# ScalarE's share of a weight conversion, put behind the ScalarE work that stands ahead of it in the source

## The chip, the cores and the metric

One core of a Trainium2 chip runs the whole program. The metric is device time in microseconds (us), the median of several runs; a lower time is better. The core has five engines that work side by side, each through its own list of instructions in the order in which it was given: TensorE (PE in the profile; its weight loads are PEld), VectorE (DVE), ScalarE (ACT), GpSimd (POOL) and SyncE (SP), which here only issues DMA transfers.

## The reference, cut to what matters

Retention over 4 batches, 8 heads, 576 positions of 64 elements, then two feed-forward layers over 2304 tokens. The four weight matrices come as 64-bit floats and are converted on the chip; the other inputs are float32.

```python
scores = q @ k.T / sqrt(64)
x = (scores * (gamma ** (i - j) where i >= j else 0)) @ v   # 2304 x 512
h = x @ moe_w_in                                            # 512 -> 2048
g = where(h > 0, h, exp(min(h, 0)) - 1)
x = g @ moe_w_out                                           # 2048 -> 512
h = maximum(x @ moe2_w_in, 0)
out = (h * h) @ moe2_w_out
```

## The kernel before, in words

**Tokens and steps.** The 2304 tokens are five blocks of 512, 512, 256, 512 and 512. The 2048 hidden columns are 16 slices `f` of 128. A step (layer, block, f) is an `up` (12 matmuls, which make `h` for one slice) and, two steps later (`LAG`), a `down` (12 matmuls, which add that slice's part to four accumulators `acc`). Each product is three matmuls (lines 130 to 132), since every operand is split into a high and a low half: ScalarE's cast (line 126) makes the high half, VectorE's subtraction (line 127) the low one. In layer one, blocks 0 and 1 take turns in three groups of slices: block 0 with f = 0 to 5, block 1 with f = 0 to 5, block 0 with f = 6 to 10, and so on; these 32 steps use each weight slice twice. The third operation behind an `up` is ScalarE's Tanh (line 314); behind it VectorE makes `t` (lines 316, 317), and ScalarE and VectorE split it into `g`, which the `down` needs.

**Weights.** A unit is one slice of one of the two matrices of a layer, 32 units in layer one (list `w1`). `load_raw` brings it in, `to_f32` converts it with two ScalarE operations (lines 160, 161) and four VectorE ones (162, 163, 164, 167), and `split_w` splits it with one cast on ScalarE and one subtraction on VectorE. `w1_to(n)` carries this on until n units are split; the source calls it after each piece of the first block's attention (`EARLY`) and in `mid`, in the middle of each `up`, behind the Tanh, with n from `units1(i)`: 7 units, then 1.4 a step, then 0.85 a step.

**Attention.** A chunk of up to 128 positions goes through `transposes` (PE line 239, then ScalarE's copies, line 244), `scores` (PE 252, then VectorE's masking, 255) and `values` (PE 267 and 271, then `x` is split, lines 126 and 127; PE 281 and VectorE 287 or 289 carry the state `st` on). `scale_chunk` is VectorE's line 214. Block 1 has five chunks: one of 64 positions (done ahead of the steps or beside the first), three of 128, of which the first starts a batch, and one of 64. `SPREAD` places their pieces in the source in the first five steps. They share two PSUM buffers (`ps_a`) and one set of `qT`, `kT`, `P0`, `P1`, and each chunk needs the state of the one before, so they follow each other nearly in series. The first `up` of block 1 needs all five.

**What sets the order.** The source is in this order, but a scheduler lays the instructions of each engine out anew when the program is built, by its own estimate of when each could start. It keeps what data needs, and edges that the source adds: `tc.issue_after(ins)` puts ScalarE's instructions of its block behind `ins`, if that is one of ScalarE's, in ScalarE's list. The conversion of layer two's weights already stands in such a block (behind `mark[0]`, the last Tanh); that of layer one doesn't.

Of the kernel before, what the change touches and what calls it, by code (L numbers as in the profile page):

```python
# [98 lines left out]
def tile_kernel(ctx: ExitStack, tc, q, k, v, w_in1, w_out1, w_in2, w_out2, cst, out):  # L99
    nc = tc.nc  # L100
# [36 lines left out]
    def load_raw(layer, which, f):  # L137
        w = ((w_in1, w_out1), (w_in2, w_out2))[layer][which].bitcast(I32)
        if layer == 0:

            t = wp.tile([P, DM, 2], I32, tag=f"w{which}_{f}", name="raw")
        else:
            t = raw_p.tile([P, DM, 2], I32, tag="raw", name="raw")
        if which == 0:
            nc.sync.dma_start(
                out=t.rearrange("p (k f) t -> p k (f t)", k=KC),
                in_=w[:, 2 * f * P:2 * (f + 1) * P].rearrange("(k p) f -> p k f", p=P),
            )
        else:
            nc.sync.dma_start(out=t.rearrange("p c t -> p (c t)"), in_=w[f * P:(f + 1) * P, :])  # L150
        raws[layer, which, f] = t
# [229 lines left out]
    w1 = [(0, *u) for u in units]  # L381
# [8 lines left out]
    at = dict(load=0, scale=0, next=0, raw=0, f32=0, split=0, raw2=0, f322=0, park=0, fetch=0, split2=0)  # L390
# [26 lines left out]
    def step(name, limit, todo_, work):  # L417
        if at[name] < min(limit, len(todo_)):
            work(todo_[at[name]])
            at[name] += 1  # L420

    def w1_to(n):

        while at["split"] < min(int(n), len(w1)):
            while at["raw"] < min(at["f32"] + AHEAD, len(w1)):
                step("raw", 99, w1, lambda u: load_raw(*u))
            step("split", at["f32"], w1, split_w)
            step("f32", at["raw"], w1, to_f32)
# [14 lines left out]
    for (c, piece), n in zip(pieces, EARLY):  # L443
        first[c][piece]()
        w1_to(n)
        if piece == 0 and c < 2:
            scale_next()
        if (c, piece) in ((0, 2), (2, 2)):
            load_next()
# [5 lines left out]
    for i, (layer, blk, f) in enumerate(steps):  # L455
        def mid():
            for of, (lo, hi) in SPREAD.items():
                if lo <= i < hi:
                    need = 3 * len(blocks[of])
                    for _ in range((i - lo + 1) * need // (hi - lo) - (i - lo) * need // (hi - lo)):  # L460
                        attn_step()
            if at["split"] < len(w1):
                w1_to(units1(i))
            elif layer == 0 and i >= SHARED and at["f322"] < min(len(w2), units2(i)):

                step("park", at["f322"], w2, park_w)
                with tc.issue_after(mark[0]):
                    step("f322", at["raw2"], w2, to_f32)
                while at["raw2"] < min(len(w2), at["f322"] + 2):
                    step("raw2", 99, w2, lambda u: load_raw(*u))  # L470
# [19 lines left out]
        if (layer, f) == (0, 1) and blk == NB - 1 or (layer, f) == (1, LAG) and blk < NB - 1:  # L490
            n = blk + 1 if layer else 0
# [30 lines left out]
```

## Time and profile before

| | |
|---|---|
| median of 3 runs | 946.06 us (943.92 to 947.9) |
| profiled execution: its time, and its span from the first to the last instruction | 946.56 us, 944.8 us |
| mean granted clock of TensorE, as a share of 2.4 GHz | 0.977 |
| busy in the span: PE, PEld, DVE, ACT | 906.6, 753.2, 506.9, 423.3 us |
| DMA, over the span | 97.47 MB, mean 103 GB/s |

The profile gives one execution. Busy time is time within instructions; those of one engine can overlap a little, so that the time that an engine needs for one more instruction is read from start to start of instructions that follow each other without a gap. Matmul ends are modelled. A mean over the span hides stages with other limits, so the stretches are read one by one.

### The profile page before, as it was taken

What the parts mean: (1) busy time and instruction counts of PE and PEld (TensorE: products, weight loads), DVE (VectorE), ACT (ScalarE), POOL (GpSimd) and SP (SyncE); (2) the same over time, 40 slices, a digit from 0 to 9 for tenths busy, and PEclk for the clock granted to TensorE, in tenths of its full rate; (3) what the DMA queues carried; (4) which work ended last, traced back from release to release, by engine and by line L of the source; (5) the groups of instructions that cost most, each with busy time, mean ns of one, the idle gap of its engine ahead of it and who ended that gap; (6) DMA issues with size and microseconds to landing.
All of it is one profiled execution on the core that took longest, in us unless ns stands there. A gap on an engine that the chain in (4) does not pass through costs nothing.

```text
span 944.8 us, 12423 instructions
## 1 busy us (share of the span) xinstructions
PE 906.6 (96%) x4934; PEld 753.2 (80%) x4934; DVE 506.9 (54%) x890; ACT 423.3 (45%) x770; POOL 9.3 (1%) x12
## 2 busy tenths in 40 slices
PE   7798589999998999999999999999999999999997
PEld 5676577887788998888788888888888988888886
DVE  5899995354557878767787642223223332223222
ACT  4797464544555666565767632222222222223221
POOL 3000000000000000000000000000000000000000
PEclk9889599999998999999999999999999999999999
DMA  9995230222148567433854530011003020001001
GB/s 230 297 369 137 46 89 1 89 90 89 45 123 253 161 168 218 139 125 110 289 196 140 153 137 1 1 44 45 1 1 134 1 112 1 1 1 45 1 1 44
DMA packets 97081, 97.47 MB, mean 103 GB/s; under 512 B 59264, under 2 KB 77824, under 8 KB 96512
## 3 DMA queue, kind: packets, MB, share of 16 engines
q1 hardware_dynamic: 97024, 96.69, 33.6%
q8 instruction: 38, 0.62, 0.3%
q14 instruction: 19, 0.16, 0.1%
HBM read 69.94 MB, written 26.74 MB: 102 GB/s over the span
## 4 chain that ended last, share of the span: by engine, by line
PE 83%; DVE 12%; DMA 2%; issue 1%; ACT 0%; SPq 0%; POOL 0%; DVEq 0%
PE acc L130 13%; PE acc L131 13%; PE h L130 13%; PE acc L132 13%; PE h L132 13%; PE h L131 13%; DVE f L164 2%; DVE f L167 2%; DVE w L127 2%; PE ps_o L271 2%; PE ps_s L252 1%; DVE f L162 1%; PE ps_o L267 1%; DVE f L163 1%; PE ps_t L239 1%
## 5 line engine op out<-in xcount | busy, mean ns | idle before, releaser
L130 PE MATMUL h<-x,w 128*128 128x512 f32 (+1 forms) x640 | 239.4, 375 | 3.8 <-DVE t L317 3.8
L131 PE MATMUL h<-x,w 128*128 128x512 f32 (+1 forms) x640 | 237.3, 371 | 0.0
L132 PE MATMUL h<-x,w 128*128 128x512 f32 (+1 forms) x640 | 237.1, 370 | 0.0
L321 DVE SCALAR_TENSOR_TENSOR t<-h,t 128x512 f32<-128x512 f32 (+1 forms) x80 | 51.1, 639 | 230.0 <-ACT t L319 230.0
L319 ACT ACTIVATE t<-h 128x512 f32<-128x512 f32 (+1 forms) x80 | 44.4, 555 | 237.2 <-PE h L132 237.2
L130 PEld LDWEIGHTS h<-x,w 128*128 128x128 f32 x640 | 122.0, 191 | 27.0 <-DVE t L317 5.3
L126 ACT CAST g<-t 128x512 fp32r<-128x512 f32 (+1 forms) x160 | 92.4, 578 | 110.1 <-DVE t L321 52.1
L127 DVE TENSOR_TENSOR g<-t,g 128x512 fp32r<-128x512 f32 (+1 forms) x160 | 102.1, 638 | 70.9 <-ACT g L126 64.8
L131 PEld LDWEIGHTS h<-x,w 128*128 128x128 f32 x640 | 122.0, 191 | 21.2 <-DVE x L127 0.4
L132 PEld LDWEIGHTS h<-x,w 128*128 128x128 f32 x640 | 121.7, 190 | 20.3
L131 PE MATMUL acc<-g,w 128*128 128x512 f32 (+1 forms) x320 | 118.7, 372 | 1.2 <-DVE g L127 1.2
L132 PE MATMUL acc<-g,w 128*128 128x512 f32 (+1 forms) x320 | 118.0, 370 | 0.0
L130 PE MATMUL acc<-g,w 128*128 128x512 f32 (+1 forms) x320 | 113.5, 378 | 0.0
L130 PE MATMUL acc<-w,g 128*128 128x512 f32 x288 | 112.2, 390 | 0.0
L131 PE MATMUL acc<-w,g 128*128 128x512 f32 x288 | 112.2, 390 | 0.0
L132 PE MATMUL acc<-w,g 128*128 128x512 f32 x288 | 111.6, 389 | 0.0
L316 DVE SCALAR_TENSOR_TENSOR t<-e,t 128x512 f32<-128x512 f32 (+1 forms) x80 | 50.9, 636 | 74.5 <-ACT t L314 74.5
L312 ACT ACTIVATE t<-h 128x512 f32<-128x512 f32 (+1 forms) x80 | 44.2, 553 | 85.7 <-PE h L132 81.7
L131 PEld LDWEIGHTS acc<-g,w 128*128 128x128 f32 x320 | 60.2, 188 | 11.8 <-DVE g L127 1.9
L130 PEld LDWEIGHTS acc<-g,w 128*128 128x128 f32 x320 | 59.3, 188 | 11.6 <-issue 0.9
L132 PEld LDWEIGHTS acc<-g,w 128*128 128x128 f32 x320 | 60.3, 188 | 10.3
L132 PEld LDWEIGHTS acc<-w,g 128*128 128x128 f32 x288 | 54.1, 188 | 11.4
(65 smaller groups left out, 936.1 us busy)
## 6 DMA issues: line engine op xcount, KB each, us to landing
raw<-in_moe_w_in_dram SPq DMA_DIRECT2D x32, 512.0 KB, 5.7
raw<-in_moe_w_out_dram SPq DMA_DIRECT2D x32, 512.0 KB, 5.9
x2s<-x SPq DMA_DIRECT2D x16, 512.0 KB, 3.6
w2s<-f SPq DMA_DIRECT2D x32, 256.0 KB, 2.3
x<-x2s SPq DMA_DIRECT2D x4, 2048.0 KB, 8.4
f<-w2s SPq DMA_DIRECT2D x32, 256.0 KB, 2.7
out_dram<-o SPq DMA_DIRECT2D x18, 256.0 KB, 2.5
parts<-part SPq DMA_DIRECT2D x8, 512.0 KB, 2.8
```

The lines of the kernel that those rows point to most:

```text
L126: nc.scalar.copy(pair_hi, src)
L127: eng.tensor_tensor(out=pair_lo, in0=src, in1=pair_hi.bitcast(F32), op=ALU.subtract)
L130: nc.tensor.matmul(ps, l_hi, r_hi, start=first, stop=False)
L131: nc.tensor.matmul(ps, l_hi, r_lo, start=False, stop=False)
L132: nc.tensor.matmul(ps, l_lo, r_hi, start=False, stop=last)
L164: nc.vector.scalar_tensor_tensor(out=ai, in0=upper, scalar=-(1 << 31), in1=ai, op0=ALU.bitwise_and, op1=ALU.bitwise_or)
L167: nc.vector.tensor_tensor(out=ai, in0=ai, in1=lower, op=ALU.add)
L271: nc.tensor.matmul(ps[e * D:(e + 1) * D, p, :n], vn[:n, 2 * p + e, :], live[e][:n, p, :n], start=not s, stop=True, skip_group_check=True,)
L312: nc.scalar.activation(t, h, AF.Relu, scale=-1.0)
L316: nc.vector.scalar_tensor_tensor(out=t, in0=e, scalar=1.0, in1=t, op0=ALU.add, op1=ALU.mult)
L319: nc.scalar.activation(t, h, AF.Relu)
L321: nc.vector.scalar_tensor_tensor(out=t, in0=h, scalar=0.0, in1=t, op0=ALU.max, op1=ALU.mult)
```

## The change

Whenever a call of `w1_to` has something to do, all that it issues stands in an `issue_after` block behind the last ScalarE instruction that the source has issued by then. In `mid` that is the Tanh of this step's `up`, or, since the attention's pieces are issued ahead of it there, the last ScalarE operation of those. Nothing is added or taken away on any engine: each has as many instructions as before.

```diff
+    def last_act():
+        return next(i for i in reversed(nc.cur_bb.bb.instructions) if i.engine == mybir.EngineType.Activation)
+
     def w1_to(n):
 
+
+        if at["split"] < min(int(n), len(w1)):
+            with tc.issue_after(last_act()):
+                w1_run(n)
+
+    def w1_run(n):
         while at["split"] < min(int(n), len(w1)):
             while at["raw"] < min(at["f32"] + AHEAD, len(w1)):
                 step("raw", 99, w1, lambda u: load_raw(*u))
```

What the scheduler makes of it is seen in the engines' lists. Names are those of tiles; in `w_5_958` the 5 is the slice, and the last number counts tiles. ScalarE from the first split of an `x` of block 1's attention on, first as it was ahead of and around the split of `w_3_627` (slice 3 of the second matrix):

```order
L161 ACTIVATE f<-raw 128x512
L160 ACTIVATE raw<-raw 128x512
L126 CAST w_4_534<-f 128x512
L160 ACTIVATE raw<-raw 128x512
L126 CAST g<-t 128x512
L160 ACTIVATE raw<-raw 128x512
L161 ACTIVATE f<-raw 128x512
L312 ACTIVATE t<-h 128x512
L160 ACTIVATE raw<-raw 128x512
L313 ACTIVATE e<-t 128x512
L126 CAST w_3_627<-f 128x512
```

and the same place, up to the same split, now:

```order
L126 CAST g<-t 128x512
L314 ACTIVATE t<-t 128x512
L312 ACTIVATE t<-h 128x512
L126 CAST g<-t 128x512
L313 ACTIVATE e<-t 128x512
L314 ACTIVATE t<-t 128x512
L126 CAST g<-t 128x512
L312 ACTIVATE t<-h 128x512
L313 ACTIVATE e<-t 128x512
L126 CAST x<-ps_o 128x4x128
L126 CAST w_3_627<-f 128x512
```

Conversions (lines 160 and 161) of later slices stood between the steps' own operations; now three steps' own operations and a chunk's `x` come ahead of them. VectorE has no edge of its own, but its list follows. The end of block 1's attention there, up to the low half of its last `x`, before:

```order
L255 TENSOR_TENSOR P_918<-ps_s,cs 64x4x64
L255 TENSOR_TENSOR P_920<-ps_s,cs 64x4x64
L214 TENSOR_TENSOR q<-q,cs 128x512
L167 ISA f<-raw,f 128x1024
L162 TENSOR_SCALAR f<-f 128x512
L127 TENSOR_TENSOR w_10_1487<-f,w_10_1487 128x512
L163 TENSOR_SCALAR f<-f 128x512
L127 TENSOR_TENSOR w_12_1534<-f,w_12_1534 128x512
L164 SCALAR_TENSOR_TENSOR f<-raw,f 128x512
L162 TENSOR_SCALAR f<-f 128x512
L127 TENSOR_TENSOR x<-ps_o,x 128x4x64
```

and now:

```order
L127 TENSOR_TENSOR w_6_849<-f,w_6_849 128x512
L162 TENSOR_SCALAR f<-f 128x512
L127 TENSOR_TENSOR g<-t,g 128x512
L163 TENSOR_SCALAR f<-f 128x512
L214 TENSOR_TENSOR k<-k,cs 128x512
L164 SCALAR_TENSOR_TENSOR f<-raw,f 128x512
L255 TENSOR_TENSOR P_918<-ps_s,cs 64x4x64
L255 TENSOR_TENSOR P_920<-ps_s,cs 64x4x64
L167 ISA f<-raw,f 128x1024
L214 TENSOR_TENSOR q<-q,cs 128x512
L127 TENSOR_TENSOR x<-ps_o,x 128x4x64
```

The same `x` now comes when slice 6 is being split, where it came when slice 12 was. On TensorE, behind the first two `up` of block 1 (`w_0_217`, `w_1_269`) there now stands block 0's `down` of slice 5, which stood ahead of block 1's first `up` before:

```order
L132 MATMUL h<-x,w_1_269 128x512
L130 MATMUL h<-x,w_1_269 128x512
L131 MATMUL h<-x,w_1_269 128x512
L132 MATMUL h<-x,w_1_269 128x512
L130 MATMUL acc_750<-g,w_5_958 128x512
L131 MATMUL acc_750<-g,w_5_958 128x512
```

Its twelve matmuls moved past the two `up`. All lists are as before again from about the 32nd step on.

## Rows read from the trace of the kernel before

**Rows 1.** The page, busy us (share of the span) and instructions of three engines.
```profile
PE 906.6 (96%) x4934; PEld 753.2 (80%) x4934; DVE 506.9 (54%) x890; ACT 423.3 (45%) x770; POOL 9.3 (1%) x12
```

**Rows 2.** Windows: start:end, length, busy us (instructions) per engine, granted clock, DMA.
```profile
core 0: us, PE busy (x) PEld busy (x) DVE busy (x) ACT busy (x) POOL busy (x), PEclk, DMA share, GB/s
44.70:117.70 73.00, 56.24 (x392) 45.11 (x390) 72.77 (x142) 52.90 (x97) 0.00 (x0) 0.82 0.63 191
46.00:88.00 42.00, 37.16 (x198) 28.73 (x199) 41.92 (x81) 36.38 (x67) 0.00 (x0) 0.92 0.85 265
88.00:117.00 29.00, 17.20 (x173) 14.99 (x171) 28.85 (x58) 15.04 (x28) 0.00 (x0) 0.69 0.31 82
116.90:132.00 15.10, 12.54 (x65) 9.97 (x64) 14.99 (x31) 9.66 (x18) 0.00 (x0) 0.92 0.33 71
146.00:288.00 142.00, 142.00 (x710) 115.42 (x709) 70.53 (x113) 68.09 (x119) 0.00 (x0) 1.00 0.26 80
318.00:456.00 138.00, 138.00 (x935) 117.33 (x931) 103.22 (x198) 84.78 (x163) 0.00 (x0) 1.00 0.54 161
```

**Rows 3.** Timeline of VectorE: start us, us, engine, line, operation, tiles, form, count.
```profile
44.71 0.68 DVE L164 SCALAR_TENSOR_TENSOR f<-raw,f 128x512 int32<-128x512 int32 x1
...
113.92 0.68 DVE L167 CUSTOM_DVE_ANT_0 f<-raw,f 128x1024 uint16<-128x1024 uint16 x1
114.52 0.41 DVE L162 TENSOR_SCALAR f<-f 128x512 f32<-128x512 f32 x1
114.86 0.68 DVE L127 TENSOR_TENSOR w<-f,w 128x512 fp32r<-128x512 f32 x1
...
117.33 0.41 DVE L127 TENSOR_TENSOR x<-ps_o,x 128x256 fp32r<-128x256 f32 x1
```

**Rows 4.** Timeline of TensorE, 46 to 118 us; in brackets idle time before, and its releaser.
```profile
46.13 0.63 PE L239 MATMUL ps_t<-cs,q 128*128 128x128 f32 x4 [0.25 <-DVE q L214]
...
69.84 0.39 PE L131 MATMUL acc<-g,w 128*128 128x512 f32 x1
70.07 0.39 PE L132 MATMUL acc<-g,w 128*128 128x512 f32 x1
...
83.66 1.16 PE L252 MATMUL ps_s<-qT,kT 64*128 64x128 f32 x16
...
88.56 1.06 PE L267 MATMUL ps_o<-qT,st 128*128 128x128 f32 x8
...
90.47 0.64 PE L281 MATMUL ps_u<-v,k 128*64 128x64 f32 x16
92.92 0.66 PE L239 MATMUL ps_t<-cs,q 128*128 128x128 f32 x4 [1.82 <-DVE x L127]
...
95.92 2.08 PE L252 MATMUL ps_s<-qT,kT 64*128 64x128 f32 x16 [1.51 <-ACT kT L244]
100.75 2.08 PE L267 MATMUL ps_o<-qT,st 128*128 128x128 f32 x8 [2.75 <-DVE P L255]
...
104.53 1.07 PE L281 MATMUL ps_u<-v,k 128*64 128x64 f32 x16
107.17 0.46 PE L239 MATMUL ps_t<-cs,q 64*128 64x64 f32 x4 [1.58 <-DVE x L127]
...
116.93 1.22 PE L130 MATMUL h<-x,w 128*128 128x512 f32 x2
```

**Rows 5.** Timeline of ScalarE, two conversions and a cast in a stretch without gaps.
```profile
52.10 0.69 ACT L160 ACTIVATE raw<-raw 128x512 int32<-128x512 uint32 x1
52.67 0.62 ACT L126 CAST w<-f 128x512 fp32r<-128x512 f32 x1
53.17 0.73 ACT L160 ACTIVATE raw<-raw 128x512 int32<-128x512 uint32 x1
```

**Rows 6.** Waits, 46 to 146 us: waiter, releaser, us in total, times, longest.
```profile
ACT w L126 <- DVE f L167: 10.0, 7, 3.4
```

## The prediction, made before the changed kernel was run

> **What bounds the kernel now.** I read the page's busy shares first, then windows of successive stretches, then the timelines of the stretch that stands out. By the page TensorE is the bound: 906.6 of 944.8 us busy, VectorE half idle [rows 1]. The windows say when that holds: from 146 to 288 us and from 318 to 456 us TensorE is busy without a gap, at a granted clock of 1.00 [rows 2]. It doesn't hold early. From 88 to 117 us TensorE is busy 17.2 of 29 us, at a mean granted clock of 0.69, so partly at the lower of its two levels (1.2 instead of 2.4 GHz), and VectorE is busy 28.85 of 29; from 44.7 to 117.7 us VectorE is busy 72.77 of 73.0 us [rows 2]. There VectorE is the bound, and the reader should ask what it is busy with.
>
> The timeline of TensorE shows what is waited for. From 92.92 us on it does only block 1's attention, chunk after chunk, at 14.25 us each (92.92 to 107.17), and stands idle in front of the transposes for VectorE's `x`, and in front of `ps_o` for VectorE's `P` (2.75 us); only at 116.93 us does block 1's first `up` begin [rows 4]. It reads the last `x`, whose low half VectorE makes at 117.33 us [rows 3]. So all that VectorE does ahead of that `x` delays TensorE, and part of it needn't be there: the lists show conversions of slices 6 to 12, while block 1's first six steps use slices 0 to 5.
>
> **What the change moves.** No instruction is added or removed. The lists of before and after are the same on VectorE up to the operation that starts at 44.71 us [rows 3]. From that place up to the last `x` of block 1, VectorE has 140 instructions before and 80 after. All but the weight conversions agree: 11 scalings, 8 maskings, 6 of state, 5 `x` and 18 for `t` and `g` in both. The 60 that moved behind are 13 of line 162, 12 of 163, 12 of 164, 11 of 167 and 12 of line 127 on weights. From start to start a full-size operation takes 0.60 us (113.92 to 114.52) and a line 162 takes 0.34 (114.52 to 114.86) [rows 3]; line 163 is like 162. So 35 x 0.60 + 25 x 0.34 = 29.5 us of VectorE's work leave the stretch, and 73.0 - 29.5 = 43 us stay. If VectorE never waited, the last `x` would come at 88 us. That is the bound on one side.
>
> ScalarE loses the matching work there (32 conversions, 12 casts, at 0.57 and 0.50 us from start to start [rows 5], 24 us); it was not full (52.90 of 73 us [rows 2]), so this counts only by what it delays.
>
> **The bound on the other side: the attention as a chain.** With VectorE's queue short, TensorE's own list decides. Between the first 128-position chunk's transposes, at 46.13 us [rows 4], and the next chunk's, it now has 3 `up` and 4 `down`, 84 matmuls, at 0.23 us from start to start (69.84 to 70.07 [rows 4]) 19.3 us, and some 4 us of attention: not before 69.5 us. VectorE comes to that chunk's scaled `q` after 22.7 us of work, at 67.4 us plus waits. I take 70 us.
>
> From there three chunks follow in series. One chunk at the full clock: two transposes 1.3, ScalarE's copy 0.6, scores 1.16, two maskings 1.3, `ps_o` 1.9 (88.56 to 90.47), ScalarE's and VectorE's `x` 1.3, together 7.6 us; at the lower clock scores 2.08, `ps_o` 3.8 (100.75 to 104.53) and transposes 1.5, together 10.6 [rows 4]. The last chunk has 64 positions; 5.5 to 7.5 us is my estimate from halved operations. TensorE's list also puts the `up` of slice 5 and the `down` of slice 4 between the pieces: 24 matmuls, 5.5 us, part of which covers copies and maskings, and the slice's own split must come first; I add 4.5. So block 1's first `up` starts 25 to 33 us after 70: between 95 and 105, taken as 100 us, against 116.93 before.
>
> **The sum.** (1) 116.9 - 100 = 16.9 us gained. (2) The `down` of slice 5, 12 x 0.23 = 2.7 us, was done by then before, and now comes after: -2.7. (3) From 116.9 to 132 us TensorE was idle 2.6 us and its granted clock was 0.92, about 1.2 us lost [rows 2]; the changed lists let block 1's `down`s find their weights ready, but I keep the clock's recovery and 1 us of thin waits: +1.6. Together 15.8 us. (4) The 29.5 us of VectorE's work come later, under the matmuls of steps 6 to 25. From 146 to 288 us VectorE was busy 70.53 of 142 us [rows 2], so 71 us lie free there, and it costs nothing while that holds; without that cover it would cost the whole gain. (5) From step 32 on nothing is reordered; those stages start earlier and take as long. SP's list moves the stores of block 0's partial sums behind eight to ten loads of later chunks. Their buffers come free with the transposes of block 2's first chunk, right behind the first two `up` of block 1, and the store is needed only by block 1's own partial sums six steps (some 33 us) later: nothing.
>
> The profiled execution took 946.56 us, span 944.8 and 1.8 around it; its time is 0.5 above the median. 946.56 - 15.8 = 930.8, and against the median 930.3. I predict **930.5 us**.
>
> **What new waits it could make.** The two conversions now stand in ScalarE's list behind a Tanh, which waits for TensorE; behind them stand the weight's cast, which waits for VectorE's four operations, and then the next `up`'s Relu. The next `up` but one needs its `h` buffer back, after ScalarE's three and VectorE's two operations. Serially these are 2.7 us, and a unit queued ahead of them on both engines adds at most 2 x 0.57 + 0.50 and 3 x 0.60 + 2 x 0.34, 4.1 us [rows 3, 5]: 6.8 us. TensorE meanwhile has two `down` and one `up`, 36 x 0.23 = 8.2 us. So 1.4 us of slack a step. What speaks for it beside the sum: layer two's conversion already stands behind the Tanh, at 0.6 units a step, and there TensorE was busy 138.00 of 138.00 us while VectorE was busy 103.22 [rows 2].
>
> **The rivals.**
> - *Nothing is gained.* By the page's shares TensorE is the bound and no work leaves it, so the time would stay at 946. For it speaks 96% [rows 1]; against it 17.2 of 29 us [rows 2]: the idle is in one place, and the change acts there. [...] Chance 0.06.
> - *Slower: ScalarE's list blocks.* If a weight's cast waits for VectorE with the next Relu behind it, longer than the 1.4 us of slack, TensorE waits in each of the 20 steps from 6 to 25. It decides from 15.8 / 20 = 0.8 us a step on: equal at 0.8, slower by 0.5% at 1.0. Casts did wait for VectorE's line 167, 7 times, 3.4 us at the longest [rows 6]; 2.0 us beyond the slack in 20 steps would give 930 + 40 = 970 us. Against it: those waits fell where VectorE had a backlog, which the change takes away. The page "PSUM — Partial Sum Buffer" of the Trainium skill, section "Engine vs sequencer instructions", says that ScalarE's and VectorE's queues are strictly first in, first out, by which a waiting cast holds the Relu even if its `h` is ready; no row here shows one overtaken. Chance 0.07.
> - *A smaller gain.* The same blocking only while block 1's attention runs: with a 3.4 us wait in two of three chunks the first `up` starts at about 107, the gain is 9 us, 937 to 941. Chance 0.09.
> - *A larger gain.* VectorE hardly waits and the chunks overlap with the `up` and `down` between them: `up` at 88 to 94 us, gain 22 to 30 less the 2.7 already counted, 917 to 925. Chance 0.10.
> - The forecast, 925 to 937 (the `up` at 95 to 105, and a thin wait more or less): 0.68.
>
> **How the numbers follow.** The forecast's range holds 0.68; the smaller gain up to 940 and the larger from 920 add about 0.13, so the range is 920 to 940. About 0.5% (4.7 us) is what a measurement of this kernel can tell from no change: faster takes the forecast, the larger and nearly all of the smaller gain, 0.87; same 0.06; slower 0.07.
>
> **What would show it.** In the changed kernel's trace: block 1's first `up` at 95 to 105 us (step 1); VectorE with gaps from 57 to 100 us, 43 us of work in some 55; TensorE without gaps, at a clock of 1.00, from 115 to 280 us, and VectorE busier than before there, by some 20 us from 146 to 288 (step 4); the same operation of a late step starting earlier by the whole gain, no more and no less (step 5). Wrong, if TensorE waits step after step for line 317 behind 130 us, or if the chunks still follow at 14 us each.

## The result and the profile after

The changed kernel takes 933.84 us (median of 4 runs, 932.09 to 935.93) against 944.99 us for the kernel before in the same session (4 runs, 943.54 to 947.9). The ratio over all these runs is 0.9879, with a 95% interval of 0.9846 to 0.9912, so it is faster by 1.2%. The profiled execution took 935.93 us, the slowest of the four, with a span of 934.2 us: 10.6 us less than before in both.

The page, busy time, answers to [rows 1]; no engine's work changed by more than 2 us:

```profile
PE 904.7 (97%) x4934; PEld 751.4 (80%) x4934; DVE 508.7 (54%) x890; ACT 422.7 (45%) x770; POOL 9.1 (1%) x12
```

The windows of the changed kernel (start:end, length, busy us of PE, PEld, DVE, ACT and POOL, granted clock, DMA share, GB/s) answer to [rows 2]:

```profile
46.00:88.00 42.00, 35.10 (x240) 28.05 (x240) 29.82 (x53) 20.82 (x38) 0.00 (x0) 0.92 0.86 261
88.00:117.00 29.00, 25.40 (x189) 20.83 (x188) 26.03 (x49) 16.52 (x33) 0.00 (x0) 0.88 0.30 68
...
104.70:119.90 15.20, 15.20 (x64) 12.46 (x63) 12.22 (x23) 12.44 (x25) 0.00 (x0) 0.86 0.42 99
119.90:260.00 140.10, 140.10 (x657) 111.08 (x656) 105.82 (x181) 89.76 (x156) 0.00 (x0) 1.00 0.27 84
...
146.00:288.00 142.00, 139.40 (x730) 113.48 (x730) 104.83 (x183) 86.91 (x157) 0.00 (x0) 0.99 0.33 101
...
318.00:456.00 138.00, 138.00 (x878) 115.92 (x877) 101.49 (x190) 84.74 (x157) 0.00 (x0) 1.00 0.56 174
...
106.00:260.00 154.00, 154.00 (x715) 122.46 (x715) 116.85 (x201) 100.90 (x177) 0.00 (x0) 0.99 0.29 86
...
452.00:490.00 38.00, 35.84 (x152) 29.22 (x151) 29.59 (x52) 25.76 (x48) 0.00 (x0) 0.96 0.60 192
```

Three rows carry the reading. From 46 to 88 us VectorE fell from 41.92 to 29.82 us of work. From 88 to 117 us TensorE rose from 17.20 to 25.40 busy us and its granted clock from 0.69 to 0.88. And from 146 to 288 us VectorE rose from 70.53 to 104.83 us, which is where the moved conversions went, while TensorE is gapless at a clock of 1.00 up to 260 us. The 2.6 us that it lacks in the row to 288 lie behind 260, at the passage to the 256-token block; the kernel before has 2.6 us of idle time at the same passage.

The timeline of TensorE in the changed kernel answers to [rows 4]:

```profile
41.10 0.39 PE L130 MATMUL h<-x,w 128*128 128x512 f32 x1
...
48.20 0.63 PE L239 MATMUL ps_t<-cs,q 128*128 128x128 f32 x4 [0.94 <-DVE q L214]
...
73.91 0.63 PE L239 MATMUL ps_t<-cs,q 128*128 128x128 f32 x4 [1.28 <-DVE q L214]
...
75.75 1.16 PE L252 MATMUL ps_s<-qT,kT 64*128 64x128 f32 x16 [0.67 <-ACT kT L244]
80.26 2.08 PE L267 MATMUL ps_o<-qT,st 128*128 128x128 f32 x8 [3.35 <-DVE P L255]
...
86.02 0.60 PE L239 MATMUL ps_t<-cs,q 128*128 128x128 f32 x4
...
97.23 0.46 PE L239 MATMUL ps_t<-cs,q 64*128 64x64 f32 x4
...
101.53 1.37 PE L267 MATMUL ps_o<-qT,st 128*128 128x64 f32 x8 [1.77 <-DVE P L255]
...
104.74 1.22 PE L130 MATMUL h<-x,w 128*128 128x512 f32 x2
...
259.98 0.28 PE L130 MATMUL h<-x,w 128*128 128x256 f32 x1
...
928.22 1.07 PE L132 MATMUL acc<-w,g 128*128 128x512 f32 x4
```

and the same operations of the kernel before, where [rows 4] don't have them:

```profile
39.73 0.39 PE L130 MATMUL h<-x,w 128*128 128x512 f32 x1
...
270.53 0.28 PE L130 MATMUL h<-x,w 128*128 128x256 f32 x1
...
938.83 1.07 PE L132 MATMUL acc<-w,g 128*128 128x512 f32 x4
```

Read one operation at a time, these give the whole account. Block 1's first `up` moved from 116.93 to 104.74: 12.2 us. The first matmul of step 32 moved from 270.53 to 259.98: 10.55 us. The last group moved from 938.83 to 928.22: 10.6 us. So 12.2 us were won ahead of block 1's first `up`, 1.6 us were given back by step 32, and behind it the difference stays the same.

One wait was new. The timelines of VectorE and of SyncE's DMA issues in the changed kernel show it; it falls between the scores at 75.75 and `ps_o` at 80.26:

```profile
76.64 0.69 DVE L214 TENSOR_TENSOR q<-q,cs 128x512 f32<-128x512 f32 x1 [2.28 <-DMA q<-in_q_dram]
78.92 0.69 DVE L214 TENSOR_TENSOR k<-k,cs 128x512 f32<-128x512 f32 x1 [1.58 <-DMA k<-in_k_dram]
79.53 1.28 DVE L255 TENSOR_TENSOR P<-ps_s,cs 128x512 f32<-128x512 f32 x2
```

```profile
67.40 3.39 SPq L150 DMA_DIRECT2D raw<-in_moe_w_out_dram  x1
...
71.37 0.52 SPq L204 DMA_DIRECT2D q<-in_q_dram  x1
72.03 1.89 SPq L204 DMA_DIRECT2D k<-in_k_dram  x1
```

VectorE, no longer backed up, arrives at the scaling of the next chunk's `q` and `k` before their loads do. The masking of the chunk in hand stands behind these scalings in its list, so TensorE waits 3.35 us for `P`. The loads were issued at 71.37 and 72.03, behind a weight load whose issue took 3.39 us. (A run with the weight loads issued earlier, further down, shortens these waits.)

### The profile page after: what moved, and what is told of

Same layout as the page of the kernel before. It is cut to its first block, busy times and chain, and to the rows that moved or that the text cites. A ratio compares the mean times of both kernels' runs of the same rounds, so it can differ in the third digit from the quotient of the medians.

```text
span 934.2 us, 12422 instructions
## 1 busy us (share of the span) xinstructions
PE 904.7 (97%) x4934; PEld 751.4 (80%) x4934; DVE 508.7 (54%) x890; ACT 422.7 (45%) x770; POOL 9.1 (1%) x12
## 4 chain that ended last, share of the span: by engine, by line
PE 89%; SPq 3%; DMA 3%; DVE 2%; ACT 1%; issue 1%; DVEq 0%
PE h L130 14%; PE acc L130 14%; PE h L132 14%; PE h L131 14%; PE acc L131 14%; PE acc L132 13%; SPq L204 2%; PE ps_o L271 2%; PE ps_s L252 1%; PE ps_o L267 1%; PE ps_t L239 1%; DMA f<-w2s 1%; DMA k<-in_k_dram 1%; DMA raw<-in_moe_w_out_dram 1%; PE ps_u L281 1%
```

## The experiments

The kernel before was timed beside each group: 946.16 us (15 runs) for the first four, 946.08 us (11 runs) for the others. Starts in us are read from the one profiled execution of each kernel. The rows above differ by 1.4 us (41.10 against 39.73) ahead of the place that the change touches, so a difference of that size between two kernels' starts is no evidence.

**Is it VectorE's list or ScalarE's that has to be short?** The first run ties the same calls on VectorE instead of ScalarE.

```diff
-    def last_act():
-        ... i.engine == mybir.EngineType.Activation)
+    def last_dve():
+        ... i.engine == mybir.EngineType.DVE)
...
-            with tc.issue_after(last_act()):
+            with tc.issue_after(last_dve()):
```

> The edge is put on VectorE instead of ScalarE: VectorE's instructions of a layer-one conversion stand behind the VectorE work ahead of them in the source; ScalarE has no edge. ScalarE's list has 32 conversion operations ahead of block 1's last x, as before the change (13 with it); VectorE's list has 43 us of work there, as with the change. Theory (what counts is VectorE's work ahead of that x): block 1's first up at 98 to 107 us, the time within 0.4% of the changed kernel, 930 to 938 us. Rival (the gain comes from ScalarE's list, its own operations no longer behind conversions): first up at 112 to 118, time 941 to 948.

939.52 us (6 runs, 934.84 to 942.43), ratio 0.9921 (0.9887 to 0.9955); block 1's first `up` at 106.69 us. The expected start is met; the median is slightly past the upper edge, and the interval overlaps with the change's. VectorE makes the low half of block 1's last `x` at 103.25 us here. The same operation in the change, and the first `up` with this edge:

```profile
104.40 0.42 DVE L127 TENSOR_TENSOR x<-ps_o,x 128x256 fp32r<-128x256 f32 x1 [1.40 <-ACT x L126]
```

```profile
106.69 0.63 PE L130 MATMUL h<-x,w 128*128 128x512 f32 x2
```

The `x` comes no later than in the change; the `up` does, because matmuls of slice 5's `down` stand in front of it on TensorE (103.20 to 106.69). So either engine's edge frees the early stretch. Why, the counts of weight casts further down show.

**Which of the edges matter?** The next two runs keep the edge for the calls of steps 0 to 5 (and of the attention ahead of them) alone, or for those from step 6 on alone.

```diff
-            with tc.issue_after(last_act()):
+            if now[0] < 6:          # the other kernel: >= 6
+                with tc.issue_after(last_act()):
+                    w1_run(n)
+            else:
                 w1_run(n)
```

> The change, but only for conversions that the source issues up to step 5; later ones are free as before the change. VectorE's list up to block 1's last x is as with the change (43 us), ScalarE's has 30 conversion operations ahead of it. Theory: the gain is made in front of that x and nowhere else; first up at 100 to 107, time 930 to 938. Rival (the edges of steps 6 to 25 earn a part, by keeping ScalarE free for the next Relu): time 938 to 944.

935.29 us (4 runs, 930.92 to 937.84), ratio 0.9871 (0.9833 to 0.9910), first `up` at 105.71: not to be told from the full change, as the theory had it.

> The change, but only for conversions that the source issues from step 6 on. VectorE's list then has 14 weight slices split ahead of block 1's last x (12 with the change, 24 before it), 4.9 us more work than with the change. Theory (VectorE's list ahead of x): first up 0 to 5 us later than with the change, time 934 to 940; the edges of the later steps do it, since those are the conversions that ran ahead. Rival (the edges that count are those of the first steps): time 941 to 948.

939.73 us (6 runs, 934.82 to 942.91), ratio 0.9921 (0.9894 to 0.9949), first `up` at 108.40, within what the theory gave. The edges of the later steps act on the early stretch too, since it is the later slices' units that had been pulled into it.

**Is it VectorE's work alone?** The kernel before, with VectorE's four conversion operations left out for the last 20 of the 32 units of layer one (ScalarE's two and the split stay, on unconverted numbers).

```diff
         nc.scalar.activation(a, upper.bitcast(F32), AF.Abs, scale=2.0 ** -112)
+        if u[0] == 0 and w1.index(u) >= 12:
+            f32s[u] = a
+            return
         nc.vector.tensor_scalar_min(a, a, MOST)
```

> The kernel before the change, without VectorE's four conversion operations for the last 20 of layer one's 32 weight slices (left out, so those weights are not converted); ScalarE's operations, the splits and the loads stay. VectorE's list has 53 us of work up to block 1's last x (72 before, 43 with the change). Theory: less work of VectorE in front of that x is enough, without any edge: first up at 98 to 108 us, time 927 to 938. Rival (VectorE's work is not what the x waits for): first up at 113 to 118, time 942 to 947.

941.77 us (8 runs, 938.79 to 945.25), ratio 0.9948 (0.9926 to 0.9971), and the first `up` at 116.65, where it was before. The theory as I had put it failed. The timeline of TensorE in this kernel, and its windows:

```profile
81.82 2.08 PE L130 MATMUL acc<-g,w 128*128 128x512 f32 x4 [3.20 <-ACT g L126]
...
100.88 2.08 PE L255 MATMUL ps_s<-qT,kT 64*128 64x128 f32 x16 [2.61 <-ACT kT L247]
```

```profile
44.70:120.00 75.30, 60.85 (x392) 48.61 (x391) 54.73 (x97) 57.58 (x109) 0.00 (x0) 0.79 0.63 190
88.00:117.00 29.00, 20.69 (x185) 17.27 (x184) 16.24 (x29) 15.04 (x30) 0.00 (x0) 0.73 0.31 82
...
46.00:106.00 60.00, 48.48 (x271) 38.01 (x272) 48.59 (x84) 54.78 (x102) 0.00 (x0) 0.82 0.67 208
```

VectorE is now busy 16.24 of the 29 us, and yet nothing comes earlier: ScalarE is busy 54.78 of the 60 us from 46 to 106, and TensorE waits for its `g` and `kT` instead. The groups of ScalarE's weight casts from 44.7 us up to block 1's last `x` say what happened, first before, then the change, the tie on VectorE, and this kernel:

```profile
L126 ACT CAST w<-f 128x512 fp32r<-128x512 f32 x19 | 11.7, 618 | 8.5 <-DVE f L167 8.5
```

```profile
L126 ACT CAST w<-f 128x512 fp32r<-128x512 f32 x8 | 5.0, 620 | 0.5 <-DVE f L167 0.4
```

```profile
L126 ACT CAST w<-f 128x512 fp32r<-128x512 f32 x9 | 5.4, 611 | 3.7 <-DVE f L167 3.7
```

```profile
L126 ACT CAST w<-f 128x512 fp32r<-128x512 f32 x27 | 16.3, 616 | 0.0
```

With VectorE's part gone, the scheduler pulled 27 units through ScalarE ahead of that `x`, against 19 before and 8 and 9 in the two tied kernels. So the run is no test of VectorE's share alone, but it tells more: units ahead of the `x` delay the attention through ScalarE's list too, once VectorE's is relieved. The tie on VectorE left 22 of ScalarE's first conversions (line 160) in front, against 5 in the change, and still gained, so it isn't these that count; what had gone from both lists there is the rest of those units. First the tie, then the change:

```profile
L160 ACT ACTIVATE raw<-raw 128x512 int32<-128x512 uint32 x22 | 14.4, 673 | 0.0
```

```profile
L160 ACT ACTIVATE raw<-raw 128x512 int32<-128x512 uint32 x5 | 3.4, 675 | 0.0
```

The first and second half of the edges alone leave 7 and 9 casts. The first half gains as much as the change; the second brings the `up` forward by 8.5 of the 12.2 us, and its 0.8% in time against 1.2% can't be told apart by the intervals.

**Do the moved conversions cost anything later?** The kernel before, with the last 19 units of layer one only loaded: conversion and split are left out on both engines, and the steps use earlier slices in their place.

```diff
         raw = raws.pop(u)
+        if u[0] == 0 and w1.index(u) >= 13:
+            f32s[u] = None
+            return
...
         layer, which, f = u
+        if f32s[u] is None:
+            w_t[u] = w_t[0, which, f % 6]
+            return
```

> The kernel before the change, in which the last 19 of layer one's 32 weight units are only loaded: their conversion and split are left out on both engines, and the steps use earlier slices in their place. Both engines' lists then have no more conversions ahead of block 1's last x than with the change, without an edge. Theory, as mended after the run that left out VectorE's part alone (conversions ahead of that x delay it on either engine, ScalarE as soon as VectorE is relieved): first up at 98 to 107 us, as with the change. Second question: what the conversions cost that the change puts under steps 6 to 25. If they are covered, the time is that of the changed kernel, 928 to 937 us; if they cost, it is faster than 926. Rival (neither engine's conversions matter, the edge does something else): first up at 113 to 118, time 941 to 947.

928.74 us (4 runs, 927.60 to 931.59), ratio 0.9821 (0.9799 to 0.9843); first `up` at 109.63, later than the 98 to 107 expected. As in the kernel before, its list has the `down` of slice 5 ahead of that `up`, 2.7 us which the change has behind it; without it the start would be at 106.9, by this estimate. The fair comparison is at step 32 and later. The windows of this kernel and its timeline of TensorE:

```profile
106.00:260.00 154.00, 153.90 (x754) 125.60 (x755) 72.01 (x111) 71.19 (x119) 0.00 (x0) 0.98 0.26 79
...
452.00:490.00 38.00, 38.00 (x170) 31.45 (x169) 15.73 (x23) 19.07 (x33) 0.00 (x0) 1.00 0.12 48
```

```profile
260.56 0.28 PE L130 MATMUL h<-x,w 128*128 128x256 f32 x1
...
921.58 1.07 PE L132 MATMUL acc<-w,g 128*128 128x512 f32 x4
```

Step 32 begins at 260.56 us here and at 259.98 in the change: doing the conversions beside steps 6 to 25 costs nothing, though VectorE is busy 116.85 us of 154 in the change and 72.01 here. The last group comes 6.6 us earlier than in the change, and that arises after step 32. Most of it lies from 452 to 490 us: there the change has TensorE busy 35.84 us, in 152 matmuls, with the DMA engines at a share of 0.60, and this kernel has 38.00 us, 170 matmuls and 0.12, and no wait. The wait there is no cost of the change, since the kernel before has it at the same operation; before, then the change:

```profile
472.75 0.50 PE L130 MATMUL h<-x,w 128*128 128x512 f32 x1 [2.07 <-DVE t L317]
```

```profile
460.75 0.80 PE L130 MATMUL h<-x,w 128*128 128x512 f32 x1 [2.16 <-DVE t L317]
```

The waits of the changed kernel from 452 to 490 us (waiter, releaser, us in total, times, longest) name what is behind it. VectorE, ahead of that `t`, waited 2.7 us for ScalarE's cast of a weight, and the cast waited for a transfer, a layer-two weight that comes back from its store `w2s`:

```profile
ACT w L126 <- DMA f<-w2s: 5.5, 5, 2.4
...
DVE w L127 <- ACT w L126: 2.7, 1, 2.7
```

**Can the new wait be taken away?** Three kernels on top of the change: the next chunk's scaling put behind the VectorE work ahead of it in the source (`issue_after(last_dve())` around `scale_next()`), weight loads allowed 8 units ahead instead of 6, and both.

```diff
             if len(todo) == 1:
-                scale_next()
+                with tc.issue_after(last_dve()):
+                    scale_next()
```

```diff
-AHEAD = 6
+AHEAD = 8
```

> The change, and one more edge: VectorE's scaling of the next chunk stands behind the maskings of the running one, in front of which it waited for its q and k (2.3 and 1.6 us) with the change. Theory (this wait is on the chain to block 1's first up): the maskings start 2 to 3 us earlier, the first up at 99 to 103 us instead of 104.7, time 928 to 934, 0.2 to 0.5% under the changed kernel. Rival (the chain finds another wait): first up at 104 to 107, time as the changed kernel, 932 to 938.

932.07 us (5 runs, 931.32 to 935.39), ratio 0.9857 (0.9838 to 0.9877), first `up` at 104.09. The timeline of TensorE in this kernel:

```profile
46.57 0.63 PE L239 MATMUL ps_t<-cs,q 128*128 128x128 f32 x4 [0.92 <-DVE q L214]
...
74.06 0.63 PE L239 MATMUL ps_t<-cs,q 128*128 128x128 f32 x4 [3.09 <-DVE q L214]
...
76.63 2.08 PE L252 MATMUL ps_s<-qT,kT 64*128 64x128 f32 x16 [0.68 <-ACT kT L244]
79.49 2.07 PE L267 MATMUL ps_o<-qT,st 128*128 128x128 f32 x8 [0.78 <-DVE P L255]
```

The wait for `P` is down from 3.35 to 0.78 us, and block 1's first `up` moves by 0.65 us: the transposes now wait 3.09 us for `q`, and the scores take 2.08 instead of 1.16 us. Even the 0.65 us are not shown to come from the edge, since the first chunk's transposes start at 46.57 here and at 48.20 in the change.

> The change with AHEAD 8 instead of 6: the weight loads are issued two units earlier, so that none stands between the loads of block 1's chunks in SP's list. Theory (the chunks' q and k were late behind the weight loads): VectorE's waits for q and k, 4.5 us together with the change, fall under 2; first up at 101 to 104, time 929 to 935. Rival (the loads of all weights in front delay the chunks by as much): waits of 4 us or more, first up at 104 to 109, time 933 to 940.

937.07 us (6 runs, 933.48 to 937.93), ratio 0.9897 (0.9877 to 0.9916), first `up` at 104.72. VectorE's waits for `q` and `k` shrink from 4.5 us to 1.1 in all (44 to 120 us); TensorE waits 2.10 us for `q` ahead of transposes that come at 75.67.

> Both of the last two: the edge for the scaling, and AHEAD 8. Theory: what is left of the wait for q and k is no longer in front of the maskings; first up at 98 to 103 us, time 926 to 933. Rival (the chain at TensorE's lower clock sets the pace): first up at 103 to 107, time 932 to 937.

937.35 us (6 runs, 935.96 to 938.52), ratio 0.9908 (0.9891 to 0.9926), first `up` at 106.46, with transposes at 77.64. VectorE has no wait for these loads left, and the `up` isn't earlier. So in all three the wait goes and the `up` starts at 104 to 107 us, where the rivals had it, because another part of the chain takes the time. The reasons that two of the rivals gave are not borne out: with the loads ahead VectorE's waits did fall under 2 us, and that the lower clock sets the pace was not shown. The first of the three is nominally the fastest kernel that computes all; its interval overlaps with the change's, so it isn't shown to be better.

## Why the prediction was right, and which term was off

The forecast was 930.5 us, within 920 to 940; 933.84 was measured. The mechanism was right: the stretch to 117 us was held by conversions that nothing needed yet, and the gain arose there alone. By its steps:

- **Term (1), block 1's first `up`, was mis-sized: 12.2 us instead of 16.9.** It came at 104.74, at the edge of the 95 to 105 that I gave, not at 100. The difference of 4.7 us splits in two. The three chunks took 30.8 us (73.91 to 104.74), 0.8 more than the 30 that I took and within 25 to 33; they follow at 12.1 and 11.2 us, against 14.25 before. The second 128-position chunk's transposes came at 73.91 instead of 70, 3.9 us. Of these, 1.4 us were there before the changed place, in this execution: the `up` matmul that is first in the rows above starts at 41.10 instead of 39.73 (from 16 to 44.7 us the granted clock was 0.82, against 0.88 before). The rest built up from there to 73.91: the first chunk's transposes waited 0.94 us for `q`, against 0.25 before, and the second's 1.28 us. I had started my sum from the 46.13 of before, as if nothing moved ahead of it, and had allowed 0.5 us for all waits up to the second chunk. The 3.35 us wait for `P` at 80.26, which the bound didn't name either, lies within the 30.8 us.
- **Terms (2) and (3), −2.7 and +1.6,** were −1.1 together; measured 10.55 − 12.2 = −1.6. With (2) as worked out, (3) was 1.1 instead of 1.6. Its two halves went apart. The thin waits vanished: TensorE is busy 15.20 of 15.20 us behind the `up`, where [rows 2] have it idle for 2.6 and I had kept 1. But the clock cost more than I had kept for it: it was 0.86 there, against 0.92, which by length times missing share is 2.1 us instead of 1.2, an estimate.
- **Term (4), the cover, held.** TensorE is busy 140.10 of 140.10 us from 119.9 to 260 at a clock of 1.00, and leaving the conversions out altogether brings step 32 no earlier (260.56). The sign that I gave for it was off without harm: VectorE gained 34 us from 146 to 288, not some 20. In busy time the 60 moved operations are 35 × 0.68 + 25 × 0.41 = 34 us [rows 3] (the 29.5 went from start to start), and the trace has 72 conversion operations of VectorE in that window, against 8 before. So they all lie there, and I had put a third of them ahead of it.
- **Term (5)** held: 10.55 us at step 32, 10.6 at the end. SyncE's list cost nothing that can be seen.
- **The rival that ends slower** needed waits in each step from 6 to 25. None is there: from 104.7 to 260 TensorE has no idle time. The Trainium skill's statement that I had cited for it ("PSUM — Partial Sum Buffer", section "Engine vs sequencer instructions": strictly first in, first out) agrees with the new wait: the scores were done by 76.91 us, and their masking started at 79.53 only, behind two scalings whose loads were late.
- **The rival that nothing is gained** fell: 11.2 us were gained with no engine's work changed by more than 2 us. The Trainium skill, page "Perfetto Trace Analysis", section "Identifying the Most-Contended Engine", names the engine with the highest occupancy as the one to optimize first, TensorE by its weight-load busy share. Over the span that is TensorE in both kernels (PEld 80%, VectorE 54%); the gain came from VectorE's list, in the stretch up to 117 us.
- **A reason that the runs corrected:** "all that VectorE does ahead of that `x` delays TensorE" is half of it. Freeing VectorE and filling ScalarE gave no earlier `up`: 116.65 against 116.93.

What bounds the early stretch now was not settled. The three kernels show that it is not the one wait for loads; VectorE is still busy 26.03 of the 29 us from 88 to 117. The chain of chunks, in parts at the lower clock, and the first 128-position chunk's late start are left as candidates, argued and not shown.

## What to carry to other kernels

An engine that is half idle over the span can still be the bound in one stretch, and an early stretch of serial work is where to look: count what stands in its list ahead of the operation that the chain waits for, and ask which of it is needed only later. Independent work that a scheduler pulls ahead fills every list that it passes: an edge on either of the two engines took whole units out of both lists here, while emptying VectorE's list alone moved the queue to ScalarE's. Before such work is moved later, look for a stretch with free time on the same engine that is as long as the work, and check it by leaving the work out.

## What the runs showed that I had not expected

- Executions of one kernel differ by several us, and the granted clock mostly goes with it: the tie on VectorE ran in 934.84 us at a mean clock of 0.987 and in 942.43 at 0.979. The difference of the clocks times the span, 0.008 × 940 = 7.5 us, is an estimate of what the clock explains of the 7.6 us between them. It isn't all: the kernel before, whose 15 runs lie within 5.1 us, ran in 943.78 and in 946.84 us at the same 0.981. Each kernel has a trace of one execution only, so where in the span the others lose the clock is not shown.
- A wait that is removed from this chain needn't shorten it. With the scaling put behind, the wait for `P` went from 3.35 to 0.78 us, but from 74 to 104 us the granted clock was 0.74, against 0.86 in the change. In that kernel the scores of one chunk took 2.08 us, behind an idle time of 3.09 ahead of its transposes; in the change, idle 1.28 us there, they took 1.16, and `ps_o` behind the wait of 3.35 took 2.08. These are single executions, and what lowered the clock was not tried.
